# Two weight tiles of a second layer loaded in halves into four work tiles

## The chip, the cores and the metric

The kernel runs on one core of one Trainium2 chip. The metric is the device time of one execution in microseconds: before the change the median of three runs is 135.07 us (134.54 to 135.18). The execution that the profiler recorded took 135.0 us; its span, from the first to the last instruction, is 133.2 us, and the other 1.8 us lie around it.

## The reference

Two stages, all in float32. The first is an attention between tokens and a small state, for 8 batches, 8 heads, 512 tokens, 32 states and a head width of 64; the second is a soft mixture of 8 experts with 4 slots each over all 4608 rows (8 batches times 512 tokens and 32 states, width 512):

```python
scores  = scale * x @ state.T ; a  = softmax(scores)  ; xread = a  @ state
scores2 = scale * state @ x.T ; a2 = softmax(scores2) ; sread = a2 @ x
x2 = concat([xread, sread]) per batch            # 4608 rows of 512
logits = x2 @ phi                                # 32 slots
d = softmax of logits over the rows   ; slot_input = d.T @ x2
h = relu(slot_input[e] @ w1[e])       ; slot_out[e] = h @ w2[e]      # e = 0..7
out = softmax of logits over the slots @ slot_out
```

Every expert's `w1` (512 by 1024) and `w2` (1024 by 512) is read once: 2 MB each, 32 MB for all. With 8 MB of `x` read and 9 MB of output written, some 51 MB pass between HBM and the core.

## The kernel before

The attention stage is one long list of steps written out by hand (`ORDER`, L29 to L57): `X.4.3` is step X of batch 4 for the third group of heads, and so on. The list alone sets the order in which each engine gets its instructions; waits between engines follow from the tiles. The loop at L637 walks it. Late in the list, in its line L55, stands the step `windows` (L613), which takes two work tiles `si_m` and has POOL clear them.

After the list come the experts. `w1_part(hf, e)` (L648) multiplies the slot inputs into one expert's half of the first layer, in the order hf 0 with e 0 to 7, then hf 1 (`h_ps`, L650). `w2_part(k, hf, e)` (L706) multiplies the result into a quarter of the second layer's columns (`so_ps`, L710): k 0 and 1 with hf 0, then k 0 with hf 1, then the rest of k 1, then k 2 and 3. Between these, `out` (L734) multiplies the slot outputs by the softmax weights (`o`, L740), ScalarE and VectorE copy the sums into an output tile (L749, L750), and SP stores it (L751), 512 KB a store; `out_st` stores the two smaller outputs of 256 KB (L769). SP waits for all stores at the end (L842).

Two kinds of buffers matter here. `big` has 43 buffers of 4 KB in each of 128 partitions (512 KB in all): the `x` tiles, the state, the weight tiles and the output tiles go through them. `half` (L172) hands out tiles of 2 KB in each partition (256 KB) from 11 buffers (`NH`): all the attention's work tiles (transposed `x`, scores, exponentials), then `si_m`, then the softmax weights `c` (L680), `h_sb`, `so_sb`, `so_r` and `out_s`.

The weights are loaded by SP alone, in a fixed order (`todo`, L101): 32 tiles of the first layer, then 32 of the second, (k, e) = (0,0), (0,1), ... (3,7), one DMA of 512 KB each. `load_w` (L111) takes a `big` buffer and issues the next ones. 26 are issued ahead of the attention's list (L633), two after step R of each batch (L323), one after the later of two steps near its end (L636, L641): these are the first 43. The other 21, from tile (1,3) of the second layer on, are issued by `w1_part` (L657), two a call, into the buffers that the first layer's tiles leave when their matmuls are done. A load issued by `load_w2` (L104) holds rows `ft` to `ft + n` of the eight row tiles of a quarter; `w2t[k, e, ft]` names each.

Of the kernel before, what the change touches and what calls it, by code (L numbers as in the profile page):

```python
# [64 lines left out]
def attention_soft_moe(ctx: ExitStack, tc: tile.TileContext, x, stT, phi, w1, w2, out_x, out_s):  # L65
# [35 lines left out]
    todo = [(1, hf, e, k) for hf in range(2) for e in range(E) for k in range(2)]  # L101
    todo += [(2, k, e, 0) for k in range(4) for e in range(E)]

    def load_w2(t, k, e, ft):  # L104
        n = t.shape[1] // P
        t = t.rearrange("p (k f) -> p k f", k=n)
        nc.sync.dma_start(t, w2[e, k, :, ft : ft + n, :])
        for i in range(n):
            w2t[k, e, ft + i] = t[:, i]

    def load_w(n):  # L111
        for _ in range(min(n, len(todo))):
            layer, hf, e, k = todo.pop(0)
            t = big.tile([P, F], F32, tag="big", name=f"w{layer}_{hf}_{e}_{k}")
            if layer == 1:
                t = t.rearrange("p (k f) -> p k f", k=2)
                nc.sync.dma_start(t, w1[hf, e, :, 2 * k : 2 * k + 2, :])
                for i in range(2):
                    w1t[hf, e, 2 * k + i] = t[:, i]
            else:  # L120
                load_w2(t, hf, e, k)
# [34 lines left out]
    with ExitStack() as actx:  # L156
# [14 lines left out]

        def half(name):  # L172
            return wk.tile([P, S], F32, tag="h", name=name, bufs=NH)

        def mtile(shape, name):
            return ps_m.tile(shape, F32, tag="ms", name=name)
# [30 lines left out]
        def xe(b, g):  # L207
            r = R[b]
            r[f"xt{g}"] = half(f"xt{b}_{g}")
            act.mul(r[f"xt{g}"], r[f"xp{g}"], 0.125)  # L210
# [17 lines left out]
        def q(b, h):  # L228
            r = R[b]
            r[f"q{h}"] = half(f"q{b}_{h}")  # L230
            r[f"qv{h}"] = r[f"q{h}"].rearrange("p (k n) -> p k n", n=NS)
            dve.transpose(r[f"q{h}"], r[f"sp{h}"])  # L232
# [26 lines left out]
        def aT(b, h):  # L259
            r = R[b]  # L260
            r[f"aT{h}"] = half(f"aT{b}_{h}")
            dve.transpose(r[f"aT{h}"], r[f"q{h}"])  # L262
# [374 lines left out]
        for i, step in enumerate(order):  # L637
            name, *args = step.split(".")
            steps[name](*map(int, args))
            if i == last:  # L640
                load_w(1)  # L641


        h_ps = [ps_s.tile([P, 512], F32, tag="sc", name=f"h_ps{i}") for i in range(2)]
# [203 lines left out]
```

## Time and profile before

| | |
|---|---|
| median of three runs | 135.07 us |
| the profiled execution | 135.0 us, span 133.2 us |
| TensorE (PE) busy | 118.0 us, 89% |
| VectorE (DVE), ScalarE (ACT), GpSimd (POOL) busy | 86.8, 78.6, 44.7 us |
| moved by DMA | 51.76 MB, mean 389 GB/s |
| weight loads on SP | 64 of 512 KB, median 10.0 us from issue to landing |
| stores on SP | 16 of 512 KB (7.6 us), 2 of 256 KB (7.0 us) |

Busy time says how long an engine had work, not whether the end waited for it. A DMA's time to landing runs from its issue by SP until its semaphore says that all of it is there; where many are in flight it is mostly time in the queue. The DMA share is the mean busy share of the core's 16 DMA engines (readings just over 1 count as full).

### The profile page before, as it was taken

The numbers are of one execution on the slowest core, as the hardware profiler recorded it, in microseconds if no ns is written. First come the engines' busy times: TensorE is split into PE (matmuls) and PEld (weight loads), VectorE is DVE, ScalarE is ACT, GpSimd is POOL, SyncE is SP. The second block draws the span as 40 slices with busy tenths as digits, with TensorE's granted clock in tenths as the row PEclk, the third lists the DMA queues.
The fourth block names the chain that finished last, engine by engine and source line by source line (L and its number), as shares of the span: only waits on it lengthen the run. The fifth ranks groups of instructions, "written<-read, shape, count | busy, mean of one in ns | idle before, by whom it ended". The sixth has DMA issues, their size and how long they took to land.

```text
span 133.2 us, 5068 instructions
## 1 busy us (share of the span) xinstructions
PE 118.0 (89%) x2112; PEld 83.6 (63%) x2112; DVE 86.8 (65%) x218; ACT 78.6 (59%) x193; POOL 44.7 (34%) x64
## 2 busy tenths in 40 slices
PE   5898999999999999999899999999997999999200
PEld 2647686787886867567677779833893575754000
DVE  2019899999999999999997575059700733416300
ACT  3149999999999989988957414100100834427300
POOL 3006273563938056088884109406100000000000
PEclk9999999999999999999999999999999999999855
DMA  3999999999999999999999986999999999999992
GB/s 85 312 408 418 421 413 419 414 413 413 416 418 413 422 412 421 417 418 413 419 411 426 406 360 235 316 422 414 416 424 416 407 426 413 411 414 418 414 414 92
DMA packets 14854, 51.76 MB, mean 389 GB/s; under 512 B 1648, under 2 KB 1904, under 8 KB 14832
## 3 DMA queue, kind: packets, MB, share of 16 engines
q1 hardware_dynamic: 14544, 50.93, 95.2%
q10 hardware_dynamic: 288, 0.52, 1.1%
q8 instruction: 16, 0.26, 0.7%
q14 instruction: 6, 0.05, 0.1%
HBM read 42.53 MB, written 8.91 MB: 386 GB/s over the span
## 4 chain that ended last, share of the span: by engine, by line
PE 40%; DVE 37%; DMA 8%; issue 4%; ACT 2%; POOL 2%; DVEq 1%; ACTq 0%; POOLq 0%
PE so_ps L710 11%; PE h_ps L650 11%; PE o L740 7%; DVE l1s L248 6%; DVE q L232 6%; DVE nm L268 6%; DVE m L237 5%; DVE aT L262 5%; DMA phi_sb<-phi_in 5%; DMA x<-x_in 3%; DVE r L253 2%; POOL q L241 2%; PE os L758 2%; PE t_ps L467 1%; PE an_ps L287 1%
## 5 line engine op out<-in xcount | busy, mean ns | idle before, releaser
L750 DVE COPY out<-o 128x512 f32<-128x512 f32 x16 | 10.3, 686 | 18.7 <-PE o L740 18.7
L241 POOL TENSOR_TENSOR q<-q,m 128x512 f32<-128x512 f32 x16 | 16.7, 1050 | 16.0 <-DVE m L237 6.2
L210 ACT ACTIVATE xt<-xt_ps 128x512 f32<-128x512 f32 x32 | 18.9, 617 | 4.9 <-PE xt_ps L205 4.8
L257 POOL TENSOR_TENSOR q<-q,r 128x512 f32<-128x512 f32 x16 | 16.7, 1048 | 8.2 <-ACT eT L295 2.3
L205 PE MATMUL xt_ps<-ident,x 128*128 128x128 f32 x128 | 18.8, 285 | 0.4 <-DMA x<-x_in 0.4
L205 PEld LDWEIGHTS xt_ps<-ident,x 128*128 128x128 f32 x128 | 14.9, 146 | 3.5 <-DMA x<-x_in 1.2
L710 PEld LDWEIGHTS so_ps<-w,h_m 128*32 128x32 f32 x512 | 13.8, 110 | 4.3 <-issue 4.2
L710 PE MATMUL so_ps<-w,h_m 128*32 128x128 f32 x512 | 15.5, 274 | 0.9 <-issue 0.9
L232 DVE STREAM_TRANSPOSE q<-sc 128x512 f32<-128x512 f32 x16 | 11.1, 695 | 7.1 <-PE sc L219 7.1
L650 PE MATMUL h_ps<-w,si_m 128*32 128x512 f32 x128 | 14.4, 594 | 0.1
L749 ACT COPY out<-o 128x512 f32<-128x512 f32 x16 | 8.6, 588 | 7.2 <-PE o L740 7.2
L273 ACT ACTIVATE e<-sc,nm 128x512 f32<-128x512 f32 x16 | 11.2, 704 | 1.2 <-DVE q L232 0.4
L650 PEld LDWEIGHTS h_ps<-w,si_m 128*32 128x32 f32 x128 | 9.1, 110 | 4.0 <-issue 2.9
L315 PE MATMUL sr_ps<-x,eT 128*32 128x64 f32 x512 | 10.5, 221 | 0.3 <-ACT eT L295 0.3
L262 DVE STREAM_TRANSPOSE aT<-q 128x512 f32<-128x512 f32 x16 | 10.7, 687 | 0.0
L248 DVE TENSOR_REDUCE l1s<-q 128x16 f32<-128x512 f32 x16 | 10.5, 655 | 0.3 <-ACT q L244 0.3
L244 ACT ACTIVATE q<-q 128x512 f32<-128x512 f32 x16 | 10.5, 655 | 0.1
L268 DVE TENSOR_REDUCE nm<-sc 128x1 f32<-128x512 f32 x16 | 10.5, 660 | 0.0
L237 DVE TENSOR_REDUCE m<-q 128x16 f32<-128x512 f32 x16 | 10.5, 659 | 0.0
L287 PE MATMUL eT_ps<-ident,e 128*128 128x128 f32 x64 | 10.0, 279 | 0.5 <-ACT e L273 0.5
L315 PEld LDWEIGHTS sr_ps<-x,eT 128*32 128x32 f32 x512 | 8.6, 110 | 2.5 <-ACT lt_all L357 0.8
L287 PE MATMUL an_ps<-ident,aT 128*128 128x128 f32 x64 | 9.9, 280 | 0.2 <-DVE aT L262 0.2
(119 smaller groups left out, 187.2 us busy)
## 6 DMA issues: line engine op xcount, KB each, us to landing
w<-w_in SPq DMA_DIRECT2D x64, 512.0 KB, 10.0
out_x<-out SPq DMA_DIRECT2D x16, 512.0 KB, 7.6
x<-x_in SPq DMA_DIRECT2D x14, 512.0 KB, 10.1
x<-x_in ACTq DMA_DIRECT2D x2, 256.0 KB, 4.8
x<-x_in SPq DMA_DIRECT2D x2, 256.0 KB, 4.5
out_s<-out_s SPq DMA_DIRECT2D x2, 256.0 KB, 7.0
stT_sb<-stT_in SPq DMA_DIRECT2D x1, 384.0 KB, 7.5
stT_sb<-stT_in SPq DMA_DIRECT2D x1, 128.0 KB, 5.6
```

Of the source, the lines that this page charges most:

```text
L205: pe.transpose(p[:, P * j : P * j + P], xb[2 * b + g // 2][:, g % 2, j, :], ident)
L210: act.mul(r[f"xt{g}"], r[f"xp{g}"], 0.125)
L232: dve.transpose(r[f"q{h}"], r[f"sp{h}"])
L237: dve.tensor_reduce(out=r[f"m1{h}"], in_=r[f"qv{h}"], axis=AX.X, op=ALU.max)
L241: pool.tensor_tensor(v, v, R[b][f"m1{h}"].broadcast_to([P, 16, NS]), op=ALU.subtract)
L248: dve.tensor_reduce(out=l1s[:, i, :, 0:1], in_=R[b][f"qv{h}"], axis=AX.X, op=ALU.add)
L262: dve.transpose(r[f"aT{h}"], r[f"q{h}"])
L268: dve.tensor_reduce(out=r[f"nm2{h}"], in_=r[f"sp{h}"], axis=AX.X, op=ALU.max, negate=True)
L287: pe.transpose(p[:, j, :], r[f"{src}{h}"][:, P * j : P * j + P], ident)
L315: pe.matmul(r["srp"][32 * g : 32 * g + 32, h, :], r[f"eT{h}"][:, j, 32 * g : 32 * g + 32], xb[2 * b + g // 2][:, g % 2, j, D * h : D * h + D],
L650: pe.matmul(h_ps[hf][32 * kt : 32 * kt + 32, :], si_m[kt // 2][:, 256 * (kt % 2) + 32 * e : 256 * (kt % 2) + 32 * e + 32], w1t[hf, e, kt], ...
L710: pe.matmul(so[k][32 * i : 32 * i + 32, :], h_m[hf][:, 256 * i + 32 * e : 256 * i + 32 * e + 32], w2t[k, e, 4 * hf + i], start=(hf == 0 an ...
```

## The change

After the step `windows` SP issues the next two weight tiles, (1,3) and (1,4) of the second layer, each as two DMAs of 256 KB into four work tiles from `half`. The calls of `load_w` that follow then begin two tiles later in `todo`, so 19 instead of 21 tiles are loaded by `w1_part`. No arithmetic changes.

```diff
@@ -172,6 +172,12 @@
         def half(name):
             return wk.tile([P, S], F32, tag="h", name=name, bufs=NH)
 
+        def load_halves(n):
+            for _ in range(n):
+                _, k, e, _ = todo.pop(0)
+                for ft in (0, 4):
+                    load_w2(half(f"w2_{k}_{e}_{ft}"), k, e, ft)
+
         def mtile(shape, name):
             return ps_m.tile(shape, F32, tag="ms", name=name)
 
@@ -639,6 +645,8 @@
             steps[name](*map(int, args))
             if i == last:
                 load_w(1)
+            if name == "windows":
+                load_halves(2)
```

## Rows read from the trace of the kernel before

**Rows 1.** The page: DMA share and GB/s in 40 slices, weight loads' issues.

```profile
DMA  3999999999999999999999986999999999999992
GB/s 85 312 408 418 421 413 419 414 413 413 416 418 413 422 412 421 417 418 413 419 411 426 406 360 235 316 422 414 416 424 416 407 426 413 411 414 418 414 414 92
...
w<-w_in SPq DMA_DIRECT2D x64, 512.0 KB, 10.0
```

**Rows 2.** Stretches of 3 us: length, engines' busy us (instructions), clock, DMA share, GB/s.

```profile
79.00:82.00 3.00, 3.00 (x34) 2.81 (x29) 2.86 (x6) 0.63 (x1) 1.81 (x2) 1.00 0.73 269
82.00:85.00 3.00, 3.00 (x34) 2.81 (x30) 0.00 (x0) 0.99 (x2) 2.63 (x4) 1.00 0.77 239
85.00:88.00 3.00, 3.00 (x30) 1.89 (x26) 0.07 (x1) 0.58 (x1) 0.00 (x0) 1.00 0.95 378
88.00:91.00 3.00, 3.00 (x32) 0.91 (x28) 2.79 (x10) 0.00 (x0) 0.60 (x1) 1.00 1.03 419
```

**Rows 3.** SP's waits, 72 to 80 us: total us, times, longest.

```profile
SPq L107 <- PE h_ps L650: 6.6, 2, 5.9
```

**Rows 4.** SP's timeline, 72 to 80 us: start, length, what.

```profile
72.48 8.24 SPq L107 DMA_DIRECT2D w<-w_in  x3
```

**Rows 5.** Weight loads in five windows: issue ns, first and last start, us to landing.

```profile
L107 SPq DMA_DIRECT2D w<-w_in x4: 327/328/328, 62.2 to 66.0; - x4
DMA to landing us min/median/max: 11.3/11.4/11.5
...
L107 SPq DMA_DIRECT2D w<-w_in x1: 327/327/327, 72.5 to 72.5; - x1
DMA to landing us min/median/max: 9.8/9.8/9.8
...
L107 SPq DMA_DIRECT2D w<-w_in x1: 328/328/328, 79.4 to 79.4; - x1
DMA to landing us min/median/max: 4.1/4.1/4.1
...
L107 SPq DMA_DIRECT2D w<-w_in x1: 881/881/881, 79.8 to 79.8; - x1
DMA to landing us min/median/max: 6.3/6.3/6.3
...
L107 SPq DMA_DIRECT2D w<-w_in x10: 327/327/382, 88.7 to 101.3; - x10
DMA to landing us min/median/max: 9.8/10.9/11.3
```

**Rows 6.** PE's timeline: the last reader of the attention's work tiles.

```profile
72.60 0.63 PE L287 MATMUL an_ps<-ident,aT 128*128 128x128 f32 x4
```

**Rows 7.** A store of 512 KB and the store of 256 KB behind it.

```profile
L751 SPq DMA_DIRECT2D out_x<-out x1: 332/332/332, 113.5 to 113.5; - x1
DMA to landing us min/median/max: 7.5/7.5/7.5
...
L769 SPq DMA_DIRECT2D out_s<-out_s x1: 481/481/481, 113.9 to 113.9; - x1
DMA to landing us min/median/max: 7.8/7.8/7.8
```

**Rows 8.** The last six stores of 512 KB.

```profile
L751 SPq DMA_DIRECT2D out_x<-out x6: 332/333/1032, 120.1 to 125.5; - x6
DMA to landing us min/median/max: 5.4/6.0/6.8
```

**Rows 9.** The end: PE's last matmuls (timeline), SP's wait for stores (waits).

```profile
122.38 1.61 PE L740 MATMUL o<-lt_all,so_r 32*128 32x512 f32 x8 [0.22 <-ACT out L749]
...
SPq L842 <- DMA out_x<-out: 5.5, 3, 3.1
```

**Rows 10.** Two stretches of 0.5 us, columns as in Rows 2.

```profile
80.50:81.00 0.50, 0.50 (x10) 0.47 (x6) 0.50 (x1) 0.00 (x0) 0.50 (x1) 1.00 0.79 213
82.00:82.50 0.50, 0.50 (x10) 0.47 (x6) 0.00 (x0) 0.18 (x1) 0.50 (x2) 1.00 0.44 148
```

## The prediction

> **What bounds the kernel now.** I read the page first, its second part before its chain of waits. The DMA engines are busy from start to end at about 415 GB/s in all but a few slices; the one hole behind the start is around slices 23 to 25, where 360, 235 and 316 GB/s stand [rows 1]. PE is busier than any other computing engine (89%) but not the last to finish: its last matmuls end at 122.38 + 1.61 = 124.0 us [rows 9], while the last store is issued at 125.5 and lands 6.8 us later, at 132.3 [rows 8], with SP waiting for stores at the end [rows 9]. A store of the same size needs less than that by itself (below), so the 6.8 us are mostly queue: the stores stand behind loads that are still in the queue. The end is set by the DMA queue, and what the queue lost, it lost in the hole. The page's chain of waits ends in PE and copies, because it stops at the instructions and does not follow the stores; the wait list of SP is what shows them.
>
> Second, the stretches around the hole. From 79 to 88 us the three rows give 269, 239 and 378 GB/s against 419 in the next one [rows 2]: 150 + 180 + 41 = 371 GB/s over 3 us, 1.11 MB, or 2.66 us at 419 GB/s. That is a little over two tiles of 0.524 MB (1.25 us each).
>
> Third, why there is a hole. SP issues load 43 at 72.48 and the next one only at 79.4 [rows 4, 5], after a wait of 5.9 us for PE's first `h_ps` matmuls [rows 3]: no `big` buffer is free until the first layer's first tile has been used. At a landing time of 10.0 us [rows 1] and 1.25 us a tile, eight loads are in flight; SP puts in one whenever one lands, so a pause of 6.9 us lets the queue run dry.
>
> **The change part by part.** *Two loads move forward, as four.* They stand on SP's queue directly behind load 43, so SP would issue them at the earliest when four of the eight in flight have landed. Those are the loads issued from 62.2 to 66.0, landing 11.4 us later [rows 5]: 73.6, 74.9, 76.2, 77.3 us. All four issues thus lie before 79.4, in SP's pause, and cost the path nothing; behind them on SP stand the 19 loads left, of which the first still waits for `h_ps` until 79.4. SP has nothing else to do there, POOL's and ACT's queues get no new instruction, and PE gets only waits for landings long past (tile (1,3) is read in the `so_ps` stretch behind 94 us; the halves land near 85).
>
> *Their buffers.* The 11 work tiles were all the attention's; the last reader of any is the transpose of the last batch's `aT`, which ends at 72.60 + 0.63 = 73.2 us [rows 6]. Whichever four buffers are handed out, they are free before 73.6: no wait is added. Those that take work tiles later do not run short: two `si_m`, four halves, three `c`, two `h_sb` make eleven, and `so_sb` and what follows take those of `si_m` and `h_sb`, whose readers are done by then. Bounds: nothing to, if a buffer came late, one us for each us after 79.4 (the third rival).
>
> *What the halves fill.* Does a half take half the time? The 256 KB store issued at 113.9 landed at 113.9 + 7.8 = 121.7, the 512 KB store before it at 113.5 + 7.5 = 121.0: 0.7 us between landings [rows 7], against 1.25 for a whole tile. I take 0.65 for each half, 2.6 us for four; both ends stand, 0.62 and 1.25. The Trainium skill (DMA: Bandwidth & Descriptors, section Bandwidth) says to batch transfers to 1 MiB or more and shows 64 KB at 32% of peak, since each carries a fixed cost. By that rule halving would waste what it fills and the sum would be near 135 (the second rival); by the measured spacing a transfer's fixed part lies beside its neighbours' bytes while the queue is full, and the sum stands.
>
> *What the queue gains.* The engines begin to run dry about 79 us now (share 0.73 over the next three [rows 2]). The halves give them 2.6 us more, to some 81.5, and the load issued at 79.4 brings its first bytes about 1.2 us later (the share is 0.79 in the half microsecond from 80.5 [rows 10]). The hole closes. The gain of the queue has two ends. Upper: the mean loss, 2.66 less 0.1 for the halves, 2.6 us. Lower: landings tell of the slowest of the 16 engines, and that one lost less. The load of 72.5 landed at 82.3, that of 79.4 at 83.5, only 1.2 later, and that of 79.8 at 86.1 [rows 5]: 2.6 later, of which 1.25 is its own work, so 1.4 us was idle there. An engine that is behind uses the hole to catch up. I take the upper end: behind the hole a lag forms again (ten loads from 88.7 on take 9.8 to 11.3 us [rows 5]; a step to 11.3 means that one engine fell back by some 1.2), so the end of the kernel before carries such a lag as well.
>
> *What is late next.* With the queue 2.6 us ahead, stores stop finding a backlog. PE's order does not change, so stores are issued when they are now. The six from 120.1 on are the test: the first landed at 120.1 + 5.4 = 125.5; 2.6 earlier would be 122.9. A lone transfer of 512 KB takes at most 4.1 us (the load of 79.4), and less, as its last part came behind the tail of the one before: first bytes after 1.2, 1.25 of transfer (the share has fallen to 0.44 from 82.0 on [rows 10]), about 0.5 to the semaphore, an estimate of 3.0. So that store lands at 123.1, not 122.9. Behind it come five of 512 KB and one of 256 KB, 6.8 us as now (132.3 less 125.5): the end is 129.9 instead of 132.3. With 4.1 it would be 131.0; with 2.5 the queue alone decides, 129.7.
>
> Sum: 132.3 - 129.9 = 2.4 us off the profiled execution's 135.0, 132.6; I add 0.2 for the ends of the queue's gain and of the lone store that lie lower (1.4 and 4.1) and say 132.8. The profiled execution stands 0.07 under the median of 135.07, so it needs no correction.
>
> **The rivals.**
>
> *Part of the gain (133.6).* The lag of the slowest engine stays, and grows by later ones, because no hole lets it catch up: the landings come forward by 1.4 only. For it: the landing at 83.5 that shows no loss. Against: a lag that forms anew in both kernels. Or the lone store takes 4.1: 131.0 at the end, 133.7.
>
> *Halves cost like wholes (134.8).* Each half occupies the queue 1.25 us: four take 5.0, twice what their bytes need, and of the 2.66 only 0.2 is left. (The skill's rule, named above, points this way.) For it: nothing in the trace but the longer issue of the 256 KB store (481 ns against 332). Against: 0.7 us between landings [rows 7].
>
> *A late buffer on SP (slower, from 135.0).* SP's queue is in order: if one of the four work tiles came free late, that half and the 19 loads behind it would stand. The point from which it decides is 79.4 us: until then there is gain, behind it the hole grows by one us for each us. Freed at 82.4, say, it costs 3 us: 138.0. Against: the last reader ends at 73.2 [rows 6], with six us to spare, so this needs a buffer that the code does not show.
>
> *The end is PE's, not the queue's (135.0).* If stores took 5.4 to 6.8 us of their own, closing the hole would move nothing. For it: PE and copies run to 124 us and the page's chain stops there. Against: 4.1 us for a load of that size in a thin queue [rows 5].
>
> **How the numbers follow.** The forecast (end limited by stores, 132.2 to 133.3) gets 0.62, part of the gain (133.3 to 134.2) 0.20, halves like wholes 0.06, PE's end 0.07, a late buffer 0.05. This kernel can tell a change of 0.5%, 0.7 us, from none: faster means below 134.4. The first two and a little of the third and fourth make 0.84 faster; the rest of those two 0.11 the same; 0.05 slower. The range 132.1 to 134.2 holds the first two.
>
> **What would show it.** Right: four issues between 73.6 and 77.5 us; DMA share near 1 from 79 to 88; the load waiting for `h_ps` still at 79.4; last weight landing 1.4 to 2.7 earlier than now; the stores from 120 on with 3 to 4.5 us to landing instead of 5.4 to 6.8; PE's end where it is. Wrong: a half issued behind 79.4; landings of halves 1.25 apart; stores that still take 6 us while the queue is thin; PE ending later than 124.0.

## The result and the profile after

The changed kernel takes 132.80 us (median of 4 executions, 132.68 to 132.96) beside 135.06 for the kernel before (134.54 to 135.18): a ratio of 0.984, 95% interval 0.9813 to 0.9868. The profiled execution took 132.96 us, its span 131.2; before it was 135.0 and 133.2. Measured again later beside the last experiments, they took 132.76 and 134.55, 0.9875 (0.9847 to 0.9903). The changed kernel repeats its time; the kernel before moved by half a microsecond between the two measurements, so the gain is 1.8 to 2.3 us. The ratios leave out four disturbed executions: 136.42 and 136.71 us of the kernel before, and 166.67 and 222.84 us of two of the variants below.

The hole in the DMA queue is gone. The page after, DMA share and GB/s in 40 slices of 3.28 us, against [rows 1]:

```profile
DMA  3899999999999999999999999999999999998993
GB/s 99 285 383 418 418 411 421 415 416 410 413 420 416 418 416 417 416 417 416 418 410 420 415 416 407 414 420 413 421 420 413 422 410 416 382 413 337 421 413 157
```

Slices 24 to 26 (counted from one, 75 to 85 us; the prediction counts from nought) now hold 416, 407 and 414 GB/s. New dips stand late, 382 and 337 in slices 35 and 37: there SP waits to issue stores (below). The stretches that answer to [rows 2] (columns as there):

```profile
79.00:82.00 3.00, 3.00 (x33) 2.81 (x28) 2.76 (x5) 0.63 (x1) 1.92 (x2) 1.00 1.04 404
82.00:85.00 3.00, 3.00 (x33) 2.81 (x28) 0.00 (x0) 0.99 (x2) 2.53 (x4) 1.00 1.05 416
85.00:88.00 3.00, 3.00 (x29) 1.78 (x24) 0.18 (x1) 0.59 (x1) 0.00 (x0) 1.00 1.02 418
```

The halves' issues, then the load issued just before them, the first load that waits for `h_ps`, the last weight load, and the last six stores, each in its own window (issue ns, first and last start, us to landing), against [rows 5] and [rows 8]:

```profile
L107 SPq DMA_DIRECT2D w<-w_in x4: 327/328/509, 73.6 to 77.5; - x4
DMA to landing us min/median/max: 7.4/8.3/9.3
...
L107 SPq DMA_DIRECT2D w<-w_in x1: 328/328/328, 72.4 to 72.4; - x1
DMA to landing us min/median/max: 9.9/9.9/9.9
...
L107 SPq DMA_DIRECT2D w<-w_in x1: 328/328/328, 79.3 to 79.3; - x1
DMA to landing us min/median/max: 6.9/6.9/6.9
...
L107 SPq DMA_DIRECT2D w<-w_in x1: 328/328/328, 99.1 to 99.1; - x1
DMA to landing us min/median/max: 9.9/9.9/9.9
...
L759 SPq DMA_DIRECT2D out_x<-out x6: 332/332/1067, 119.9 to 125.4; - x6
DMA to landing us min/median/max: 3.5/4.2/4.9
```

All four halves are issued in SP's pause, and the load behind them still goes out at 79.3. The load of 72.4 lands at 82.3, the last half at 77.5 + 7.4 = 84.9: 2.6 us for four halves, 0.65 each. The last weight load, issued at 99.1 and landing 9.9 us later, is there at 109.0. In the kernel before it was this one:

```profile
L107 SPq DMA_DIRECT2D w<-w_in x1: 327/327/327, 101.3 to 101.3; - x1
DMA to landing us min/median/max: 9.8/9.8/9.8
```

It was there at 111.1. So the loads are 2.1 us ahead at their end, and the last store lands at 125.4 + 4.9 = 130.3 instead of 132.3. PE did not move much: its last matmuls (against [rows 9]) start at 122.15 instead of 122.38.

```profile
122.15 1.61 PE L748 MATMUL o<-lt_all,so_r 32*128 32x512 f32 x8 [0.22 <-ACT out L757]
```

### The profile page after: what moved, and what is told of

Its sections match the earlier page's. It is cut to its first block, busy times and chain, and to the rows that moved or that the text cites. A ratio compares the mean times of both kernels' runs of the same rounds, so it can differ in the third digit from the quotient of the medians.

```text
span 131.2 us, 5071 instructions
## 1 busy us (share of the span) xinstructions
PE 117.9 (90%) x2112; PEld 83.0 (63%) x2112; DVE 86.6 (66%) x218; ACT 78.8 (60%) x193; POOL 44.8 (34%) x64
## 4 chain that ended last, share of the span: by engine, by line
PE 52%; DVE 29%; DMA 5%; issue 4%; ACT 3%; SPq 1%; DVEq 1%; ACTq 0%
PE so_ps L718 11%; PE h_ps L658 11%; PE o L748 7%; DMA x<-x_in 5%; DVE q L238 5%; DVE aT L268 4%; DVE l1s L254 4%; DVE m L243 4%; DVE nm L274 4%; PE xt_ps L211 4%; PE an_ps L293 2%; PE eT_ps L293 2%; DVE r L259 2%; PE sr_ps L321 2%; PE sc L225 2%
```

## The experiments

Two theories were put against each other. **Queue**: the end was set by the DMA queue, and the change filled its hole. **Stores**: once the queue is ahead, the end is the issue of the last six stores by SP plus the time that they need by themselves. They can both hold, one behind the other. Rivals were a gain from the work tiles as such, and an end that is PE's.

**One tile instead of two.**

```diff
             if name == "windows":
-                load_halves(2)
+                load_halves(1)
```

> One tile, (1,3), is loaded early in two halves instead of two tiles in four. If the gain is the hole in the DMA queue that gets filled, one tile of 1.25 us fills half of it: a hole of about 1.4 us stays between 79 and 88 us, the DMA share there is about 0.9, and the time is 133.7 us (133.4 to 134.1). If the gain had nothing to do with the hole (fewer loads left for the first layer's calls, a different order of the buffers), one tile would bring either all of it (132.8) or nothing (135.0).

Measured: 133.18 us beside 134.49, 0.9894 (0.9854 to 0.9934), 1.3 us less: one tile's time in the queue. The time lies below the range expected (133.4 to 134.1), which started from a kernel before of 135.06. Its stretches of 3 us, from the slowest of its six executions (134.40), show half of the hole:

```profile
79.00:82.00 3.00, 3.00 (x33) 2.81 (x29) 2.90 (x6) 0.63 (x1) 1.52 (x2) 1.00 0.98 363
82.00:85.00 3.00, 3.00 (x34) 2.81 (x29) 0.26 (x1) 0.99 (x2) 2.93 (x4) 1.00 0.91 332
85.00:88.00 3.00, 3.00 (x29) 2.03 (x20) 0.00 (x0) 0.59 (x1) 0.00 (x0) 1.00 0.96 363
```

56 + 87 + 56 = 199 GB/s under 419 over 3 us, 1.4 us of queue, as expected. So half of the filling leaves half of the hole, and a gain of nothing is refuted. Whether one tile brings less than two, the time alone does not tell: the intervals overlap (0.9847 to 0.9903 for two). By the medians the second tile brought some 0.5 us more; the last experiments give a reason why it brought less than the first.

**The same halves, issued late.**

```diff
-            if name == "windows":
-                load_halves(2)
...
     def w1_part(hf, e):
...
             load_w(2)
+            if hf == 0 and e == 0:
+                load_halves(2)
```

> The same four halves in the same work tiles, but issued behind the first two loads that wait for the first h_ps matmuls, so at 79.4 us or later: SP's pause from 72.5 to 79.4 stays. If only the early issue matters, the hole stays and the time is 134.5 to 135.1 us. If work tiles as further buffers are what helps (loads in flight that no longer wait for the first layer's tiles), it is near 133. If the late-buffer rival had its price right, an issue at 79.4 costs nothing and gains nothing against the kernel before.

Measured: 134.69 beside 134.49, 1.0014 (0.999 to 1.0039): no gain and no loss. SP's wait list from 70 to 82 us (total, times, longest) and two of its stretches show the pause and the hole as they were:

```profile
SPq L107 <- PE h_ps L656: 7.0, 2, 6.4
```

```profile
79.00:82.00 3.00, 3.00 (x33) 2.83 (x29) 2.90 (x6) 0.63 (x1) 1.55 (x2) 1.00 0.75 257
82.00:85.00 3.00, 3.00 (x33) 2.83 (x29) 0.23 (x1) 0.99 (x2) 2.90 (x4) 1.00 0.81 251
```

The four halves went out after the pause:

```profile
L107 SPq DMA_DIRECT2D w<-w_in x4: 382/383/422, 81.0 to 82.4; - x4
```

So it is the moment of the issue that pays, not the work tiles nor the halves. The price that the late-buffer rival put on a wait behind 79.4 us was not tried: SP did not stand for a work tile here.

**Three tiles.** `h_sb` moves to two dead tiles so that six halves fit.

```diff
-            h_sb[hf] = half(f"h_sb{hf}")
+            h_sb[hf] = wk.tile([P, S], F32, tag=("st", "srN")[hf], name=f"h_sb{hf}", bufs=1)
...
-                load_halves(2)
+                load_halves(3)
```

> Three tiles in six halves; h_sb moves to two other dead tiles, with no other edit. The changed kernel's DMA share is full from 76 to 91 us, so by the queue theory a third tile finds no hole to fill: 132.5 to 133.1 us, no change against 132.8. If early loads pay for themselves whatever the queue does, 0.6 to 1.2 us more: 131.6 to 132.2.

Measured: 132.85 us, 0.9879 (0.9847 to 0.9911) of the kernel before: the time of two tiles. The third tile brought the queue hardly further ahead: the last weight load, issued at 98.7 with 10.0 us to landing, is there at 108.7, beside 109.0 with two. A queue that is full has nothing to fill. The floor that the last experiments show would have hidden most of a gain as well.

**The last two stores in halves.**

```diff
-                nc.sync.dma_start(ox, ot)
+                if (k, q) == (3, 1):
+                    for i in range(2):
+                        nc.sync.dma_start(ox[:, i], ot[:, i])
+                else:
+                    nc.sync.dma_start(ox, ot)
```

> The changed kernel with the last two stores of 512 KB each cut into two of 256 KB, each half issued once its own copy is done. If the end is the queue of the slowest DMA engine, which is never empty, no change: 132.7 to 133.0 us. If the end is the stores' own time from issue to landing, as my forecast had it, the last bytes start some 0.3 to 0.6 earlier and the last piece is half as long: 132.2 to 132.5.

Measured: 132.98 us, 0.9885 (0.9854 to 0.9917): no change, as a queue of the slowest engine that is never empty would have it. Its four small stores:

```profile
L762 SPq DMA_DIRECT2D out_x<-out x4: 512/710/916, 124.6 to 127.2; - x4
DMA to landing us min/median/max: 2.9/3.1/3.6
```

They land from 124.6 + 3.6 = 128.2 to 127.2 + 2.9 = 130.1, 0.6 to 0.7 apart, the time of a half in the queue. But each also holds SP for 0.5 to 0.9 us, so the last piece is issued at 127.2 rather than 125.4: what the shorter last piece could give, the extra issues take. Both readings fit, and this run does not tell the two theories apart.

**The kernel before with two loads left out**, and **the changed kernel with one left out.**

The edit of the first; in the second it is `[:-1]`, and tile (3,7) is read from (3,6):

```diff
-    todo += [(2, k, e, 0) for k in range(4) for e in range(E)]
+    todo += [(2, k, e, 0) for k in range(4) for e in range(E)][:-2]
...
             w2t[k, e, ft + i] = t[:, i]
+            if (k, e) == (3, 5):
+                w2t[3, 6, ft + i] = w2t[3, 7, ft + i] = t[:, i]
```

> The kernel before with the last two weight loads, (3,6) and (3,7), left out; their matmuls read tile (3,5), so the result is another. PE does the same work at the same times and the hole stays. If the end of the kernel before is set by the DMA queue, two loads less are 2.5 us of queue less and it ends as early as the changed kernel: 132.5 to 133.2 us. If its end is set by PE and the copies, 135.0.

> The changed kernel with the last weight load, (3,7), left out; its matmuls read tile (3,6), so the result is another. If the end of the changed kernel is now the stores' own issue and landing (my forecast: the first of the last six finds the queue empty), 1.25 us less in the queue brings at most 0.2: 132.6 to 132.9. If the slowest engine's queue still sets the end, it brings 0.7 to 1.1: 131.7 to 132.1.

Measured, beside 135.06 for the kernel before: 133.67, 0.9877 (0.9823 to 0.9931), with two left out of it; 132.64, 0.9826 (0.9778 to 0.9875), with one left out of the changed kernel. The first refutes an end set by PE (135.0): with PE's work unchanged the end came 1.4 us earlier. But 2.5 us of queue gave only 1.4 (132.5 to 133.2 was expected), and 1.25 us off the changed kernel gave 0.2, where the queue theory alone wanted 0.7 or more; the interval of the second still allows 0.7. The last six stores show more. First the kernel before with two loads left out:

```profile
L753 SPq DMA_DIRECT2D out_x<-out x6: 332/332/971, 121.2 to 126.5; - x6
DMA to landing us min/median/max: 2.9/3.6/4.4
```

and the changed kernel with one left out:

```profile
L761 SPq DMA_DIRECT2D out_x<-out x6: 332/332/1006, 120.0 to 125.3; - x6
DMA to landing us min/median/max: 2.9/3.6/4.4
```

In both the first of the six lands 2.9 us after its issue (the least of the six), and the end follows 6.8 us later: 121.2 + 2.9 + 6.8 = 130.9 and 120.0 + 2.9 + 6.8 = 129.7. That is what the stores theory forecasts. With two left out, PE happened to be late in the execution shown (133.76 us): its `h_ps` matmuls began at 79.4 us instead of 78.2, and the first of the six stores went out 1.1 later than before, which took that much of the gain. Two of its other executions took 132.56 and 132.82 us, near the whole of what the two loads were worth; whether PE was on time there is not recorded.

**The changed kernel again, with three loads left out of it, and the kernel before with a smaller buffer pool.** The second is the edit as before with `[:-3]`, tiles (3,5) to (3,7) being read from (3,4); the edit of the third:

```diff
-NBIG = 43
+NBIG = 42
```

> The changed kernel as it is, beside the two others of this call: 0.984 of the kernel before, as measured.

> The changed kernel with the last three weight loads left out (their matmuls read tile (3,4), so the result is another), 3.7 us less in the queue. Leaving out one load brought the landing of the last store from 130.24 to 129.7 us and its time from 132.8 to 132.6, between my two theories. If the stores' own issue and landing lie just under the queue, three loads less bring no more than one did: 0.3 to 0.9 us under the changed kernel of this call, with the first of the last six stores landing 2.4 to 3.0 us after its issue and 6.9 us more to the end. If the queue sets the end alone, they bring 2.5 to 3.7 us.

> The kernel before with 42 instead of 43 big buffers: one load less can be issued ahead of the first layer, so SP's pause begins 1.25 us sooner. By the queue theory the hole grows by one tile and the end comes 1.0 to 1.3 us later than the kernel before. If the hole is not what the change repaired, no change.

Measured, beside 134.55: the changed kernel 132.76, 0.9875 (0.9847 to 0.9903); with three loads left out 132.37, 0.9844 (0.9815 to 0.9872); with 42 buffers 135.81, 1.008 (1.0052 to 1.0108).

Three loads, 3.7 us of queue, brought 0.4 us (not clear of noise), as the stores theory had it; the queue alone would have brought 2.5 or more. Its last six stores, then the store before them and the first of the six:

```profile
L762 SPq DMA_DIRECT2D out_x<-out x6: 332/332/1005, 120.3 to 125.7; - x6
DMA to landing us min/median/max: 3.0/3.6/4.4
...
L762 SPq DMA_DIRECT2D out_x<-out x1: 338/338/338, 116.2 to 116.2; - x1
DMA to landing us min/median/max: 5.9/5.9/5.9
...
L762 SPq DMA_DIRECT2D out_x<-out x1: 332/332/332, 120.3 to 120.3; - x1
DMA to landing us min/median/max: 3.0/3.0/3.0
```

120.3 + 3.0 + 6.8 = 130.1, and 125.7 + 4.4 is the same. So behind the queue stands a floor, and by the medians the changed kernel is within half a microsecond of it. PE sets it by when it lets SP issue the stores: SP waits for VectorE's copies, and those wait for PE. In the changed kernel, SP's waits from 118 us on, and the page's line of the copies:

```profile
SPq L759 <- DVE out L758: 5.6, 4, 3.7
...
L758 DVE COPY out<-o 128x512 f32<-128x512 f32 x16 | 10.3, 686 | 18.6 <-PE o L748 18.6
```

The slowest of the later executions of the changed kernel (133.48 us) bears this out. PE was late there, its `h_ps` matmuls at 612 ns each instead of 592 (granted clock 0.938 on average, 0.977 in the first profile). The six went out from 121.2 on, over a microsecond late, the first took 2.8 us, and the last landed at 126.6 + 4.2 = 130.8.

```profile
L759 SPq DMA_DIRECT2D out_x<-out x6: 332/332/950, 121.2 to 126.6; - x6
DMA to landing us min/median/max: 2.8/3.4/4.2
```

In these four executions the end comes 9.6 to 9.8 us after the issue of the first of the six, wherever that lies. But the queue was not quite gone in any of them. With three loads left out the store before lands at 116.2 + 5.9 = 122.1 and the first of the six at 123.3, 1.2 later, a store's own time in the queue, and so it is in the other three. The trace has 16 completions for each transfer, one per DMA engine: 15 of that first store's lie at 122.7 to 122.9, the last at 123.3. So one engine was still behind, and some 0.3 us of this floor is its lag and not the stores' own time.

The smaller pool came out 1.26 us slower, the size forecast, but its hole is not larger by a tile. Its stretches, then two of its loads behind the hole, and its last six stores:

```profile
76.00:79.00 3.00, 2.85 (x44) 1.95 (x37) 1.92 (x10) 0.40 (x1) 0.00 (x0) 1.00 0.84 344
79.00:82.00 3.00, 3.00 (x33) 2.81 (x29) 2.90 (x6) 0.63 (x1) 1.55 (x2) 1.00 0.51 179
82.00:85.00 3.00, 3.00 (x33) 2.81 (x29) 0.22 (x1) 0.99 (x2) 2.89 (x4) 1.00 1.01 401
...
130.00:133.00 3.00, 0.00 (x0) 0.00 (x0) 0.00 (x0) 0.00 (x0) 0.00 (x0) 0.50 0.35 143
...
L107 SPq DMA_DIRECT2D w<-w_in x2: 387/390/392, 82.0 to 82.5; - x2
DMA to landing us min/median/max: 7.3/8.4/9.6
...
L751 SPq DMA_DIRECT2D out_x<-out x6: 332/333/977, 120.2 to 125.5; - x6
DMA to landing us min/median/max: 6.2/6.8/7.7
```

75 + 240 + 18 = 333 GB/s are missing over 3 us, 1.0 MB, no more than the 1.1 of the kernel before: it starts sooner, but the queue is back to full at 82 us already, where the kernel before needed until 88. The end is late all the same: from 130 on the mean engine has 0.35 of 3 us left, while the last store, issued at 125.5 with 7.7 to landing, lands at 133.2. A few engines finish some 2 us behind the others: of the 16 completions of that store the middle one is at 131.0 and the last at 133.3. The landings show where they fell behind. The loads of 82.0 and 82.5 land at 89.3 and 92.1, 2.7 apart by the trace where a tile takes 1.25, and those of 98.1 and 99.3 (9.9 and 11.4 us to landing) again 2.7. These two steps, 1.4 to 1.5 us each, lie behind the hole; in the hole itself the slowest engine lost some 0.6 us, less than the 1.4 of the kernel before. So this run agrees with the number and not with the mechanism as I put it. What made the steps was not tested, and the number is no support for the queue theory.

None of the variants beats the changed kernel with the whole work done.

## Why the prediction was right

The forecast was 132.8 us and the time is 132.80, but two of its terms were off and cancelled. By its steps:

- *What bounds the kernel: the queue, not PE.* Right. Leaving out two loads sped the kernel before up with the same PE work, and the same halves issued after the pause did nothing.
- *Four issues at 73.6 to 77.3, no wait for buffers, the load behind at 79.4.* Right: 73.6 to 77.5, and 79.3. SP's wait list from 72 to 80 us, against [rows 3], has the wait for `h_ps` down from 6.6 us to 1.0, and SP waits for landings instead:

```profile
SPq L107 <- DMA w<-w_in: 5.2, 7, 0.8
SPq L107 <- PE h_ps L658: 1.0, 2, 0.8
```

- *A half takes 0.65 us.* Right, 2.6 us for four: the stretches with the halves keep 404 and 416 GB/s. The Trainium skill (DMA: Bandwidth & Descriptors, section Bandwidth) says to batch transfers to 1 MiB or more, beside a table of transfers that were issued from GpSimd. The trace does not agree for 256 KB from SP in a full queue.
- *The queue gains 2.6 us, the mean loss.* Too much: the loads ended 2.1 earlier, between the two ends given (1.4 and 2.6). In this pair of executions the hole itself was worth the lower end, 1.4, to the slowest engine. Most of the rest is a step that the kernel before takes later: its loads of 88.7 and 90.0 us land at 98.9 and 101.2 by the trace, 2.3 apart where a tile takes 1.25. The changed kernel's largest step behind 82 us is 0.5. So the reason for taking the upper end, a lag that forms anew in either kernel, holds, but the two lags differ.

```profile
L107 SPq DMA_DIRECT2D w<-w_in x2: 327/327/327, 88.7 to 90.0; - x2
DMA to landing us min/median/max: 10.1/10.7/11.3
```

- *The first of the last six stores finds the queue empty, takes 3.0, lands at 123.1; the end at 129.9.* Near, but not so. No row stood behind the 0.5 us to the semaphore in the 3.0. The shortest times measured, 2.8 to 3.0 in four executions, still hold the lag of one engine; the other 15 were done with that store 2.6 us after its issue (three loads left out). In the profiled execution this store took 3.5 and plainly stood behind the one before it. These rows show it: the store before and this store, then the two microseconds from 119 on:

```profile
L759 SPq DMA_DIRECT2D out_x<-out x1: 341/341/341, 115.8 to 115.8; - x1
DMA to landing us min/median/max: 6.4/6.4/6.4
...
L759 SPq DMA_DIRECT2D out_x<-out x1: 333/333/333, 119.9 to 119.9; - x1
DMA to landing us min/median/max: 3.5/3.5/3.5
```

```profile
119.00:120.00 1.00, 0.76 (x7) 0.56 (x4) 0.90 (x2) 0.94 (x2) 0.00 (x0) 1.00 0.71 289
120.00:121.00 1.00, 1.00 (x10) 0.41 (x9) 0.39 (x1) 0.67 (x3) 0.00 (x0) 1.00 0.67 274
```

  The landings are 122.2 and 123.4, 1.2 apart, which is a store's own time in the queue: the last engine had no gap, although the engines together were idle for a third of these two microseconds. So here the slowest engine's queue set the end, 130.3, some 0.5 above the floor. The term of the queue was 0.5 too large, and the 0.2 that I added for the lower ends, with PE 0.2 earlier, made up for most of it. The profiled execution took 132.96, 0.2 more than forecast; that the median meets the forecast to the last digit is luck.
- *The rivals.* Halves that cost like wholes: refuted by their landings. An end that is PE's: refuted for the kernel before, and half true of the changed one, whose floor is set by PE. A late buffer: did not occur, and its price was not tried. Part of the gain through the slowest engine: it is what took 0.5 of the 2.6.

## What to carry to other kernels

Look for a hole in the DMA share of a kernel whose stores end behind its compute, find the wait on the issuing queue that made it, and fill it with loads into whatever buffers are dead by then; tiles cut in halves filled it at nearly the full rate here. Price it as the bytes missing in the hole, at most: the slowest engine can have lost less there. Stop at the next floor, the issue of the last stores plus the first one's time and the bytes behind it. To find that floor, leave loads out until the time no longer moves.

## What was not expected of the hardware

The mean share of the DMA engines and the landing of a transfer tell different things: a transfer has landed when its last engine is done, and engines were up to 2 us apart (with 42 buffers, share 0.35 over 130 to 133 us with the last landing at 133.2). In the changed kernel a mean share of 0.7 from 119 to 121 us hid an engine that had no gap at all. An engine that falls behind in a full queue stays behind: with 42 buffers the landings went on 1.25 us apart after each step.

A queue that has run dry does not always come back in the same time: the kernel before needed from 79 to 88 us to be full again ([rows 2]), the one with 42 buffers only until 82. In the kernel before, the second load after the pause held SP for 881 ns ([rows 5]). What decides this was not found.
